# Padding the last tile of an MLP's inner layer to 128, first loads moved to ScalarE's ring, jumps moved to the ends of the queues

## Chip, cores and metric

The kernel runs on one core of a Trainium2 chip. The metric is the device time of one execution, in microseconds (us), as the median of several. Most executions of one kernel lie within a few tenths of a per cent of each other (the widest spread here is pad_jumps', 4.8 us of 1384, 0.34%).

## The reference

```python
mod = (silu(c) @ w_mod).reshape(1, 6, 1, 640)          # six modulation rows
sa, ca, ga, sb, cb, gb = ...
# attention: x is 2048 x 640, 32 heads of 128, K and V come from a cache of 2048 rows a head
#   q = h @ wq ; p = softmax(q k^T / sqrt(128)) ; o = p v ; out = o @ wo
# mixer MLP (on 640 columns):
#   x1 = x + shifted(gelu(layernorm(x) @ w1)) @ w2
#   out = x1 + gelu(layernorm(x1) @ w3) @ w4            # w3: 640 x 1728, w4: 1728 x 640
```

Two facts matter. The inner size of the MLP is 1728 = 13 x 128 + 64, so its last tile is half a tile. And before the first attention step can run, the modulation rows, the normalised and transposed first 512 rows of x (hT of chunk 0), wq of head 0, and K and V of head 0 must all be there.

## The kernel before

A planner written in Python puts every operation into the queue of one of five engines, in the order of keys given with each operation. A DMA is also an instruction in the queue of the engine that issues it: a load "on ScalarE" stands in ScalarE's queue between its ordinary work (in before two such issues took 0.39 and 0.54 us of it, see its timeline below). The functions the argument touches (cuts marked):

```python
# jumps: how many instructions each engine executes before its jump to the unrolled code
# (a negative number counts from the end of its queue)
FIRST = {"PE": 3, "ACT": 10000, "DVE": 0, "POOL": 7, "SP": -5}
HINT  = {"PE": 0, "ACT": -30, "DVE": 0, "POOL": 0, "SP": -12}
...
def load_v(h, prio, eng="SP", gate=(), need=()):        # 512 KB: 16 x 128 rows of 256 bytes
    dma(eng, lambda e: e.dma_start(V_ap[b][:, :, 0:128],
        A_v_cache[0, h].rearrange("(t p) d -> p t d", p=128)), 512, gate, (V[b],), prio, need)
...
dma("ACT", lambda e: e.dma_start(pre_ap, mod_src(2)), 800, (wm[1],), pre_t, -292)   # "pre": w_mod part 2
load_v(0, -290, "ACT", gate=(wm[1],))                                              # V of head 0
...                                                     # V of heads 1 to 3, wq, most of x, all K: on SyncE
def w3_part(ch, key):
    for f in range(NF):                                 # NF = 14; FS[13] = 64
        fs = FS[f]
        for kk in range(KT):                            # KT = 5
            PE: matmul(m[0:fs, :], w3_ap[:, kk, f*128 : f*128+fs], nT_ap[ch][:, kk, :])
        ACT: gT_ap[0:fs, f, :] = gelu(m[0:fs, :])
def w4_tile(t, key):
    for hf in range(2):
        for f in range(NF):
            PE: matmul(m[:, ...], gT_ap[0:fs, f, ...], w4_ap[f][0:fs, hf*HD:(hf+1)*HD])
```

## Time and profile before

| | before |
|---|---|
| median of the first three runs | 1391.6 us (1391.36 to 1391.62) |
| span of the profiled execution | 1391.3 us |
| TensorE busy | 1379.4 us, 99% |
| first S matmul, first P.V matmul | 18.11, 21.77 us |
| seventh query projection starts | 64.01 us |
| last output tile starts | 1384.17 us |

The page's first table and its chain of waits:

```profile
span 1391.3 us, 29861 instructions
...
PE 1379.4 (99%) x13128; PEld 941.2 (68%) x13128; DVE 539.6 (39%) x1401; ACT 1101.5 (79%) x1143; POOL 100.9 (7%) x88
...
PE 97%; DVE 1%; DMA 1%; SPq 0%; issue 0%; ACT 0%
```

TensorE is the limit nearly all the time. What can be won is where it stands, or is slow though busy. It stands only near the start. The timeline of TensorE there (start, duration, engine, line, operation, tiles, shapes, count, and in brackets the idle time before it with what ended it):

```profile
11.74 0.29 PE L448 MATMUL f_M<-f_s_bf,f_W 128*128 128x1 bf16 x6
13.38 0.25 PE L448 MATMUL f_M<-f_s_bf,f_W 128*128 128x1 bf16 x4 [1.34 <-issue]
...
14.85 2.34 PE L666 MATMUL f_M<-f_hT,f_wq 128*128 128x512 bf16 x5 [0.64 <-DVE f_hT L568]
...
18.11 0.59 PE L734 MATMUL f_S<-f_PQ,f_KV 128*128 128x512 bf16 x2
...
21.77 0.62 PE L753 MATMUL f_O<-f_KV,f_PQ 128*128 128x129 bf16 x8
...
49.17 0.61 PE L753 MATMUL f_O<-f_KV,f_PQ 128*128 128x129 bf16 x8 [1.94 <-DMA f_KV<-in_A_v_cache_dram]
55.84 1.24 PE L666 MATMUL f_M<-f_hT,f_wq 128*128 128x512 bf16 x5
64.01 1.24 PE L666 MATMUL f_M<-f_hT,f_wq 128*128 128x512 bf16 x5
```

Ten small matmuls are cut by 1.34 us in which TensorE waited for nothing that the profile shows ("issue"). Each step (one head, 512 rows of x) has one query projection (L666); two of them are 8.17 us apart when nothing is late (55.84 to 64.01, the sixth and the seventh). At 49.17 TensorE waited 1.94 us for a V. The chain of waits, in order of time, says whose and why (start, duration, what; SPq is SyncE's queue; L573 are transposes of hT):

```profile
38.59 0.99 SPq L573
...
43.04 1.26 SPq L583
44.35 4.69 DMA f_KV<-in_A_v_cache_dram
```

It is V of head 3, which was issued only when SyncE's transposes were through.

Near the end TensorE never idles, but the tiles with a 64-row matmul take longer. The timeline of the last output tiles, and TensorE's weight loads in the list of waits (total us, times, longest):

```profile
1379.95 4.29 PE L928 MATMUL f_M<-f_KV,f_OO 128*128 128x320 bf16 x28
1384.17 4.29 PE L928 MATMUL f_S<-f_KV,f_OO 128*128 128x320 bf16 x28
...
PEld f_M L928 <- issue: 7.0, 25, 0.4
PEld f_S L928 <- issue: 2.6, 10, 0.3
```

From tile to tile it is 4.22 us for 28 matmuls (1384.17 - 1379.95). The view merges them; two of each 28 have 64 rows.

### The profile page before, as it was taken

To read this page: it belongs to the slowest core of one execution; us is meant where nothing else is said; L and a number is where in the kernel's file an instruction comes from. 1 tells how busy PE (TensorE), PEld (TensorE's weight loads), DVE (VectorE), ACT (ScalarE), POOL (GpSimd) and SP (SyncE) were. 2 spreads that over 40 slices of the span, in tenths; PEclk is the share of its full clock that TensorE was granted. 3 is DMA by queue.
4 is the path that set the end of the run, shared out by engine and by line. 5 is a ranking of instruction groups with operands and counts; after the bars stand their busy time and mean duration, and the time that the engine had idled before them with its cause. 6 is when DMAs were issued, how large, how long until landed. Compare 5 with 4: busy or idle time off the path is not lost.

```text
span 1391.3 us, 29861 instructions
## 1 busy us (share of the span) xinstructions
PE 1379.4 (99%) x13128; PEld 941.2 (68%) x13128; DVE 539.6 (39%) x1401; ACT 1101.5 (79%) x1143; POOL 100.9 (7%) x88
## 2 busy tenths in 40 slices
PE   9999999999999999999999999999999999999999
PEld 6667767777777777777777776777776766645554
DVE  5453232333233322333233323332333245987553
ACT  5888888888888898888888888888888888732222
POOL 0000000000000000000000000000333248200000
PEclk9999999999999999999999999999999999999999
DMA  9651623161214221241205122612254102531210
GB/s 220 130 115 31 117 78 83 36 107 35 46 36 84 58 46 36 48 92 30 54 17 98 31 45 36 107 36 46 55 91 114 17 16 48 120 53 24 53 43 25
DMA packets 259179, 88.90 MB, mean 64 GB/s; under 512 B 236705, under 2 KB 257762, under 8 KB 259042
## 3 DMA queue, kind: packets, MB, share of 16 engines
q1 hardware_dynamic: 255762, 84.59, 30.7%
q10 hardware_dynamic: 3280, 2.33, 0.7%
q8 instruction: 105, 1.72, 0.5%
q14 instruction: 32, 0.26, 0.1%
HBM read 43.48 MB, written 2.62 MB: 33 GB/s over the span
## 4 chain that ended last, share of the span: by engine, by line
PE 97%; DVE 1%; DMA 1%; SPq 0%; issue 0%; ACT 0%
PE f_O L753 33%; PE f_S L734 31%; PE f_M L666 10%; PE f_M L691 10%; PE f_M L928 3%; PE f_S L914 2%; PE f_O L914 2%; PE f_S L928 2%; PE f_S L887 1%; PE f_S L864 1%; PE f_O L864 1%; PE f_M L887 1%; DMA f_W<-in_w_mod_dram 0%; DMA f_KV<-in_A_v_cache_dram 0%; SPq L573 0%; PE f_M L610 0%
## 5 line engine op out<-in xcount | busy, mean ns | idle before, releaser
L736 ACT ACTIVATE f_PQ<-f_S 128x1024 bf16<-128x1024 f32 x1024 | 1041.0, 1023 | 148.2 <-PE f_S L734 135.1
L753 PEld LDWEIGHTS f_O<-f_KV,f_PQ 128*128 128x128 bf16 x8192 | 589.4, 98 | 233.7 <-issue 2.4
L734 PE MATMUL f_S<-f_PQ,f_KV 128*128 128x512 bf16 x2048 | 726.9, 379 | 0.2 <-ACT f_PQ L736 0.2
L753 PE MATMUL f_O<-f_KV,f_PQ 128*128 128x129 bf16 x8192 | 713.0, 220 | 2.7 <-DMA f_KV<-in_A_v_cache_dram 1.9
L699 DVE TENSOR_TENSOR f_y<-f_M,f_y 128x320 f32<-128x320 f32 x192 | 94.3, 491 | 536.3 <-PE f_M L691 536.3
L691 PE MATMUL f_M<-f_wo,f_OO 128*128 128x320 bf16 x992 | 272.9, 299 | 0.0
L734 PEld LDWEIGHTS f_S<-f_PQ,f_KV 128*128 128x128 bf16 x2048 | 196.7, 97 | 30.5 <-ACT f_PQ L736 1.2
L666 PE MATMUL f_M<-f_hT,f_wq 128*128 128x512 bf16 x640 | 177.3, 381 | 1.1 <-DVE f_hT L568 0.6
L691 PEld LDWEIGHTS f_M<-f_wo,f_OO 128*128 128x128 bf16 x992 | 96.1, 98 | 28.5
L762 DVE TENSOR_TENSOR f_OO<-f_O,f_rl 128x256 bf16<-128x256 f32 x256 | 108.4, 423 | 8.1
L669 DVE CAST f_PQ<-f_M 128x512 bf16<-128x512 f32 x128 | 88.5, 691 | 56.9 <-PE f_M L666 56.8
L520 POOL TENSOR_TENSOR f_y<-f_y,f_mod 128x640 f32<-128x640 f32 x32 | 49.6, 1560 | 820.1 <-DVE f_y L699 819.9
L666 PEld LDWEIGHTS f_M<-f_hT,f_wq 128*128 128x128 bf16 x640 | 62.2, 98 | 65.9 <-DVE f_hT L575 1.5
L760 DVE RECIPROCAL f_rl<-f_O 128x2 f32<-128x2 f32 x256 | 43.4, 169 | 32.1 <-PE f_O L753 27.9
L928 PE MATMUL f_M<-f_KV,f_OO 128*128 128x320 bf16 (+1 forms) x308 | 47.1, 300 | 0.0
L917 ACT ACTIVATE f_OO<-f_O 128x512 bf16<-128x512 f32 (+1 forms) x28 | 16.6, 596 | 38.5 <-PE f_O L914 38.5
L526 ACT ACTIVATE f_xn<-f_y,f_small 128x640 bf16<-128x640 f32 x10 | 9.1, 915 | 41.6 <-DVE f_small L505 41.6
L928 PEld LDWEIGHTS f_M<-f_KV,f_OO 128*128 128x128 bf16 (+1 forms) x308 | 28.6, 97 | 18.7 <-issue 7.0
L697 DVE COPY f_y<-f_M 128x320 f32<-128x320 f32 x32 | 15.7, 490 | 63.5 <-PE f_M L691 63.5
L481 DVE BATCH_NORM_STATS2 f_small<-f_y 128x6 f32<-128x320 f32 x64 | 29.6, 480 | 2.0 <-POOL f_y L520 2.0
L917 ACT ACTIVATE f_OO<-f_S 128x512 bf16<-128x512 f32 (+1 forms) x28 | 16.7, 595 | 13.1 <-PE f_S L914 13.1
L942 DVE TENSOR_TENSOR f_y<-f_M,f_y 128x640 f32<-128x640 f32 x10 | 8.2, 825 | 43.2 <-PE f_M L928 43.2
(134 smaller groups left out, 513.9 us busy)
## 6 DMA issues: line engine op xcount, KB each, us to landing
f_KV<-in_A_v_cache_dram SPq DMA_DIRECT2D x31, 512.0 KB, 4.8
f_wo<-in_A_wo_dram SPq DMA_DIRECT2D x8, 640.0 KB, 4.4
f_xin<-in_A_x_dram SPq DMA_DIRECT2D x15, 320.0 KB, 4.6
f_wq<-in_A_wq_dram SPq DMA_DIRECT2D x7, 640.0 KB, 4.6
f_W<-in_w_mod_dram SPq DMA_DIRECT2D x3, 800.0 KB, 4.9
out_dram<-f_xin SPq DMA_DIRECT2D x15, 160.0 KB, 1.8
f_KV<-in_B_w_dram SPq DMA_DIRECT2D x5, 432.0 KB, 3.3
f_KV<-in_A_k_cache_dram SPq DMA_TRANSPOSE x128, 2.7
```

What stands on the lines that cost most here:

```text
L520: P.op(eng, lambda e: e.tensor_tensor(out=out, in0=a, in1=b, op=op), COST[eng][0], rd, wr, prio, lat=300 if eng == "POOL" else None)
L666: P.op("PE", lambda e, i=i, kk=kk: e.matmul(m.ap, wq_t[g % 2][:, kk, hh * 128:(hh + 1) * 128], hT_t[ch][:, kk, :], start=(i == 0), stop=(i ...
L669: P.op("DVE", lambda e: e.tensor_copy(q.ap, m.ap), 690, (m,), (q,), s * NP - 90)
L691: P.op("PE", lambda e, m=m, qt=qt, hf=hf, hh=hh: e.matmul(m[:, 0:HD], OT_ap[gs][:, qt, hh, :], wo_t[g % 2][:, hh, hf * HD:(hf + 1) * HD], ...
L699: P.op("DVE", lambda e, m=m, yt=yt: e.tensor_tensor(out=yt.ap, in0=m[:, 0:HD], in1=yt.ap, op=ALU.add), 490, (m, yt), (yt,), s * NP - 60)
L734: P.op("PE", lambda e, sp=sp, r=r, kt=kt: e.matmul(sp[:, r * QC:(r + 1) * QC], K_ap[b][:, kt * 128:(kt + 1) * 128], q.ap, start=True, stop ...
L736: x = P.op("ACT", lambda e, sp=sp, pt=pt: e.activation(pt.ap.rearrange("p k q -> p (k q)"), sp.ap, ACT.Exp, scale=SCALE), 1021, (sp,), (pt ...
L753: ins = e.matmul(o[bk][:, w * 129:w * 129 + 129], pt[:, r, qt * 128:(qt + 1) * 128], V_ap[b][:, u, 0:129], start=(u == 0 and w == 0), stop ...
L760: P.op("DVE", lambda e, ov=ov, i0=i0: e.reciprocal(rl_t[:, i0:i0 + 2].unsqueeze(2), ov[:, 0:258].rearrange("p (u d) -> p u d", u=2)[:, :, ...
L762: evac.append(P.op("DVE", lambda e, ov=ov, i0=i0, bk=bk: e.tensor_tensor(out=On_ap[gs][:, 2 * bk:2 * bk + 2, hh, :], in0=ov[:, 0:258].rear ...
L914: P.op("PE", lambda e, m=m, f=f, kk=kk, fs=fs: e.matmul(m[0:fs, :], w3_ap[:, kk, f * 128:f * 128 + fs], nT_ap[ch][:, kk, :], start=(kk == ...
L928: P.op("PE", lambda e, f=f, hf=hf, fs=fs: e.matmul(m[:, hf * 512:hf * 512 + HD], gT_ap[0:fs, f, i * 128:(i + 1) * 128], w4_ap[f][0:fs, hf ...
```

## The change

Its intent: (1) pad the inner layer to 14 x 128, so that no matmul has 64 rows; (2) get the first data in earlier by putting plain loads on ScalarE's ring and leaving SyncE the transposes; (3) move the engines' jumps so that the gap they are taken to cause doesn't fall into the start. The diff, cut to its core:

```diff
-    FIRST = {"PE": 3, "ACT": 10000, "DVE": 0, "POOL": 7, "SP": -5}
-    HINT = {"PE": 0, "ACT": -30, "DVE": 0, "POOL": 0, "SP": -12}
+    FIRST = {"PE": 100000, "ACT": 100000, "DVE": -6, "POOL": 100000, "SP": -5}
+    HINT = {"PE": -300, "ACT": -30, "DVE": -60, "POOL": -1, "SP": -12}
...  (the planner's DMA model and some costs: cut)
+        if ch == 1:                                  # x of chunk 1 in one load, on ScalarE
+            dma("ACT", lambda e: e.dma_start(y_t[:, 4:8, :]..., x2d[512:1024, :]...), 640, (), xs + held, -296.7, after=(wm_load[3], ln0[1]))
...
-    dma("ACT", lambda e: e.dma_start(pre_ap, mod_src(2)), 800, (wm[1],), pre_t, -292)
+    dma("ACT", lambda e: e.dma_start(pre_ap, mod_src(2)), 800, (wm[3],), pre_t, -297, after=(ln0[0],))
-         modulation(2, hf, ..., lambda k, hf=hf: (-262, 0.5)[hf] + 0.01 * k, -50)
+         modulation(2, hf, ..., lambda k, hf=hf: 0.5 + hf + 0.01 * k, -50)
-    load_v(0, -290, "ACT", gate=(wm[1],))
+    load_v(0, -296.5, "ACT", after=(ln0[1],))
+        if h in (1, 2, 3):
+            load_k(h, (-294, -291, -289)[h - 1], (wm[2],), () if h < 3 else from_slot(12))
+            load_v(h, (-293, -290, -289.5)[h - 1], "ACT" if h == 1 else "SP", ...)
-    load_wq(0, 1, HG, -295.985, gate=(wm[2],))
+    load_wq(0, 1, HG, -296.8, eng="ACT", after=(ln0[0],))
...
+    pad = T()
+    P.op("POOL", lambda e: e.memset(w3_ap[:, :, FF:FP], 0.0), 300, (), (pad,) + kv(2, 3, 4), E + 12)
+    P.op("DVE", lambda e: e.memset(w4_ap[NF - 1][FL:128, :], 0.0), 400, (), (pad,) + kv(4), E + 12, slack=500.0)
...
-            fs = FS[f]
-                ... e.matmul(m[0:fs, :], w3_ap[:, kk, f * 128:f * 128 + fs], nT_ap[ch][:, kk, :], ...
+                ... e.matmul(m.ap, w3_ap[:, kk, f * 128:(f + 1) * 128], nT_ap[ch][:, kk, :], ...
-                ... e.matmul(m[...], gT_ap[0:fs, f, ...], w4_ap[f][0:fs, ...], ...
+                ... e.matmul(m[...], gT_ap[:, f, ...], w4_ap[f][:, ...], ...
...  (order of the tail: three priorities and one list: cut)
```

"ScalarE's ring" stands here for the loads that ScalarE issues; their packets have one DMA queue to themselves in the trace (q10). It now carries, in this order: pre, wq of heads 1 to 3, x of chunk 1 (below: x1), V of head 0, V of head 1.

More of the change, by code (lines that the diff above doesn't have):

```diff
@@ L93, in schedule @@
         t_eng = {e: 0.0 for e in self.ENG}
-        dma_t = 0.0
+        dma_t = {e: 1600.0 for e in self.ENG}
         avail = {e: [] for e in self.ENG}
@@ L139, in schedule @@
             if o.dma:
-                dma_t = max(dma_t, s + o.dur) + o.kb * 1024 / 340.0
-                o.end = dma_t + 2000.0
+                t = max(dma_t[e], s + o.dur)
+                both = min(max(0.0, max(dma_t[x] for x in self.ENG if x != e) - t), o.kb * 1024 / 190.0)
+                dma_t[e] = t + both + (o.kb * 1024 - 190.0 * both) / 380.0
+                o.end = dma_t[e] + 2000.0
             else:
@@ L273, in fast_path @@
     FL = FF - (NF - 1) * 128
-    FS = [128] * (NF - 1) + [FL]
+    FP = NF * 128
     G4 = D // 4
@@ L365, in fast_path @@
     W3_OFF = 2 * KVW
-    w3_ap = KV_t[:, W3_OFF:W3_OFF + KT * FF].rearrange("p (k n) -> p k n", k=KT)
+    w3_ap = KV_t[:, W3_OFF:W3_OFF + KT * FP].rearrange("p (k n) -> p k n", k=KT)
     w3 = [T() for _ in range(KT)]
-    W4_HI = W3_OFF + KT * FF
+    W4_HI = W3_OFF + KT * FP
     NW4 = 12
@@ L415, in fast_path @@
     wm = [T() for _ in range(KT)]
+    wm_load = []
     for k in range(KT):
-        dma("ACT" if k % 2 else "SP", lambda e, k=k: e.dma_start(wm_ap[:, k, :], w_mod[k * 128:(k + 1) * 128, 0:2 * D]), 320, (), (wm[k],), -300 + 0.1 * k)
+        wm_load.append(dma("ACT" if k % 2 else "SP", lambda e, k=k: e.dma_start(wm_ap[:, k, :], w_mod[k * 128:(k + 1) * 128, 0:2 * D]), 320, (), (wm[k],), -300 + 0.1 * k))
     P.op("ACT", lambda e: e.preload_act_table_set(EXPSET), 1300, (), (), -295)
@@ L486, in rstd_act @@
         P.op("ACT", lambda e: e.activation(r, mv_ap[g][:, a:b, 1], ACT.Ln, bias=EPS), 220, tuple(mvs[g][a:b]), (rs[g],), prio, slack=slack)
-        P.op("ACT", lambda e: e.activation(r, r, ACT.Exp, scale=-0.5), 220, (rs[g],), (rs[g],), prio)
+        return P.op("ACT", lambda e: e.activation(r, r, ACT.Exp, scale=-0.5), 220, (rs[g],), (rs[g],), prio)
     def rstd_dve(g, a, b, prio):
@@ L514, in normed @@
                                               op0=ALU.subtract, op1=ALU.mult),
-             430 if fp else 240, (src_t, mvs[g][i], rs[g]), (dst_t,), prio)
-    COST = {"POOL": (1600, 950), "DVE": (825, 430)}
+             445, src_t + (mvs[g][i], rs[g]), (dst_t,), prio)
+    COST = {"POOL": (1600, 950), "DVE": (825, 590)}
     def tt(eng, out, a, b, op, rd, wr, prio):
@@ L532, in scaled @@
                  (src_t, rs[g], mvs[g][i]), (out_t,), prio)
-    XP, XS = (0, -294, -20, -20), (0, -1, 22, 44)
+    XP, XS = (0, -294.5, -20, -20), (0, -1, 22, 44)
+    ln0 = []
     def ln1(ch, prio):
         g = ln_slot()
-        xs = x0 if ch == 0 else load_x2(4 * ch, XP[ch], from_slot(XS[ch])) + load_x2(4 * ch + 2, XP[ch], from_slot(XS[ch]))
+        if ch == 1:
+            xs = tuple(T(y_t[:, t, :].bitcast(BF16)[:, 0:D]) for t in range(4, 8))
+            held = tuple(v for t in range(4, 8) for v in y[t])
+            dma("ACT", lambda e: e.dma_start(y_t[:, 4:8, :].bitcast(BF16)[:, :, 0:D], x2d[512:1024, :].rearrange("(t p) d -> p t d", p=128)),
+                640, (), xs + held, -296.7, after=(wm_load[3], ln0[1]))
+        else:
+            xs = x0 if ch == 0 else load_x2(4 * ch, XP[ch], from_slot(XS[ch])) + load_x2(4 * ch + 2, XP[ch], from_slot(XS[ch]))
+            held = ()
         for a, z in ((0, 2), (2, 4)) if ch < 2 else ((0, 4),):
             for i in range(a, z):
-                ln_stats(xs[i].ap, (xs[i],), g, i, prio, 0.0 if ch == 0 else 2000.0)
+                ln_stats(xs[i].ap, (xs[i],) + held, g, i, prio, 0.0 if ch == 0 else 2000.0)
             if ch == 0:
-                rstd_act(g, a, z, prio - 100)
+                ln0.append(rstd_act(g, a, z, prio - 100))
             else:
@@ L547, in ln1 @@
             for i in range(a, z):
-                normed(xn[i].ap, xn[i], xs[i].ap, xs[i], g, i, False, prio - 1)
+                normed(xn[i].ap, xn[i], xs[i].ap, (xs[i],) + held, g, i, False, prio - 1)
         raw = [T() for _ in range(4)]
@@ L576, in ln1 @@
                                                            scalar2=saT[:, k:k + 1], op0=ALU.mult, op1=ALU.add),
-                     210, tuple(raw) + (saT, caT), (hT[ch][k],), prio)
+                     400, tuple(raw) + (saT, caT), (hT[ch][k],), prio)
     def load_k(h, prio, gate=(), need=()):
@@ L583, in load_k, with load_v, load_wq @@
             dmaT(lambda e, i=i: e.dma_start_transpose(K_ap[b][:, i * 512:(i + 1) * 512].unsqueeze(1), A_k_cache[0, h, i * 512:(i + 1) * 512, :]),
-                 128, gate if i or h else (), (K[b][i],), prio + 0.01 * i, need)
-    def load_v(h, prio, eng="SP", gate=(), need=()):
+                 128, gate if i or h else (), (K[b][i],), prio + (1.6 if h == 0 and i else 0) + 0.01 * i, need)
+    def load_v(h, prio, eng="SP", gate=(), need=(), after=()):
         b = h % NKV
-        dma(eng, lambda e: e.dma_start(V_ap[b][:, :, 0:128], A_v_cache[0, h].rearrange("(t p) d -> p t d", p=128)), 512, gate, (V[b],), prio, need)
-    def load_wq(g, a, b, prio, need=(), gate=()):
-        dma("SP", lambda e: e.dma_start(wq_t[g % 2][:, :, a * 128:b * 128],
+        dma(eng, lambda e: e.dma_start(V_ap[b][:, :, 0:128], A_v_cache[0, h].rearrange("(t p) d -> p t d", p=128)), 512, gate, (V[b],), prio, need, after)
+    def load_wq(g, a, b, prio, need=(), eng="SP", after=()):
+        dma(eng, lambda e: e.dma_start(wq_t[g % 2][:, :, a * 128:b * 128],
                                         A_wq[:, (g * HG + a) * 128:(g * HG + b) * 128].rearrange("(k p) d -> p k d", p=128)),
-            160 * (b - a), gate, tuple(wq[g % 2][a:b]), prio, need)
+            160 * (b - a), (), tuple(wq[g % 2][a:b]), prio, need, after)
     def load_wo(g, prio, need=()):
@@ L600, in fast_path @@
     of_step = lambda s: (s // (NC * HG), s // HG % NC, s % HG)
-    load_wq(0, 0, 1, -297)
-    load_k(0, -296, gate=(wm[2],))
+    load_wq(0, 0, 1, -298)
+    load_k(0, -297.5, gate=(wm[2],))
     ln1(0, -280)
@@ L617, in fast_path @@
     pre_t = tuple(K[NKV - 1]) + (V[NKV - 1],)
-    dma("ACT", lambda e: e.dma_start(pre_ap, mod_src(2)), 800, (wm[1],), pre_t, -292)
+    dma("ACT", lambda e: e.dma_start(pre_ap, mod_src(2)), 800, (wm[3],), pre_t, -297, after=(ln0[0],))
     for hf in range(2):
-        modulation(2, hf, pre_ap, pre_t, "O%d" % hf, lambda k, hf=hf: (-262, 0.5)[hf] + 0.01 * k, -50)
+        modulation(2, hf, pre_ap, pre_t, "O%d" % hf, lambda k, hf=hf: 0.5 + hf + 0.01 * k, -50)
     v_ones(NKV - 1)
-    load_v(0, -290, "ACT", gate=(wm[1],))
+    load_v(0, -296.5, "ACT", after=(ln0[1],))
     def load_head(h):
@@ L627, in load_head @@
         n = first * NP - 14 if h < HG else (first - 12) * NP
-        load_k(h, pr, (wm[2],) if h == 1 else (), from_slot(n))
-        load_v(h, pr + 1, gate=(wm[2],) if h == 1 else (), need=from_slot(n + 1))
+        if h in (1, 2, 3):
+            load_k(h, (-294, -291, -289)[h - 1], (wm[2],), () if h < 3 else from_slot(12))
+            load_v(h, (-293, -290, -289.5)[h - 1], "ACT" if h == 1 else "SP", () if h == 1 else (wm[2],), after=(ln0[1],) if h == 1 else ())
+            return
+        load_k(h, pr, need=from_slot(n))
+        load_v(h, pr + 1, need=from_slot(n + 1))
     def load_group(g):
@@ L648, in fast_path @@
                        lambda k, i=2 * n + hf: NP * (MS + i) + 4.65 + k, NP * MS - 60)
-    TAIL = ("A0 B0 B1 A1 B2 B3 WO B4 B5 I3 A2 B6 C0 B7 D0 D1 D2 B8 D3 B9 C1 D4 A3 B10 B11 "
+    TAIL = ("A0 B0 B1 A1 B2 B3 WO B4 B5 I3 A2 B6 C0 B7 D0 D1 D2 B8 B9 D3 C1 A3 B10 B11 D4 "
             "B12 D5 B13 D6 B14 D7 B15 C2 D8 D9 D10 D11 C3 D12 D13 D14 D15").split()
@@ L653, in fast_path @@
     QUAD = (2, 3)
-    WOD, CH, I3D = -100, -1000, -200
+    WOD, CH, I3D = -200, -1000, 100
     evac, last_ot = [], []
@@ L838, in fast_path @@
     for k, old in ((0, kv(2)), (1, kv(2)), (2, kv(2, 3)), (3, kv(3)), (4, kv(3, 4))):
-        dma("SP", lambda e, k=k: e.dma_start(w3_ap[:, k, :], B_w3[k * 128:(k + 1) * 128, :]), 432, (), (w3[k],) + old, E + 5 + k)
+        dma("SP", lambda e, k=k: e.dma_start(w3_ap[:, k, 0:FF], B_w3[k * 128:(k + 1) * 128, :]), 432, (), (w3[k],) + old, E + 5 + k)
     for i, (f0, f1, old) in enumerate(((0, 6, kv(0)), (6, 12, kv(0, 1)))):
@@ L911, in w3_part @@
             m = Tile(pool="T")
-            fs = FS[f]
             for kk in range(KT):
-                P.op("PE", lambda e, m=m, f=f, kk=kk, fs=fs: e.matmul(m[0:fs, :], w3_ap[:, kk, f * 128:f * 128 + fs], nT_ap[ch][:, kk, :],
+                P.op("PE", lambda e, m=m, f=f, kk=kk: e.matmul(m.ap, w3_ap[:, kk, f * 128:(f + 1) * 128], nT_ap[ch][:, kk, :],
                                                                     start=(kk == 0), stop=(kk == KT - 1)),
-                     MM(QC), (w3[kk],) + tuple(nT[ch]), (m,), key + f + 0.1 * kk, accum=True)
-            P.op("ACT", lambda e, m=m, f=f, fs=fs: e.activation(gT_ap[0:fs, f, :], m[0:fs, :], GELU),
+                     MM(QC), (w3[kk], pad) + tuple(nT[ch]), (m,), key + f + 0.1 * kk, accum=True)
+            P.op("ACT", lambda e, m=m, f=f: e.activation(gT_ap[:, f, :], m.ap, GELU),
                  act(QC), (m,), (gT[f],) + (tuple(a for b in On + OT for a in b) if ch == 0 else ()), key + f)
@@ L926, in w4_tile @@
             for f in range(NF):
-                fs = FS[f]
-                P.op("PE", lambda e, f=f, hf=hf, fs=fs: e.matmul(m[:, hf * 512:hf * 512 + HD], gT_ap[0:fs, f, i * 128:(i + 1) * 128],
-                                                                 w4_ap[f][0:fs, hf * HD:(hf + 1) * HD], start=(f == 0), stop=(f == NF - 1)),
-                     MM(HD), (gT[f], w4_of(f), w4b), (m,), key + hf + 0.01 * f, accum=True)
+                P.op("PE", lambda e, f=f, hf=hf: e.matmul(m[:, hf * 512:hf * 512 + HD], gT_ap[:, f, i * 128:(i + 1) * 128],
+                                                                 w4_ap[f][:, hf * HD:(hf + 1) * HD], start=(f == 0), stop=(f == NF - 1)),
+                     MM(HD), (gT[f], w4_of(f), w4b, pad), (m,), key + hf + 0.01 * f, accum=True)
             if last:
```

## The prediction

> What bounds the kernel now. The first table has TensorE busy 1379.4 of 1391.3 us (99%); the chain of waits that ended last is 97% TensorE. ScalarE (79%), VectorE (39%) and DMA are not the limit on average. The change can only win (a) TensorE time that is slow though busy, (b) the few places where TensorE stands.
>
> (a) The MLP's inner size is 1728 = 13 x 128 + 64. In the groups by shape the 64-row matmuls take 307 ns against 300, but in the list of waits their weight loads have 9.6 us of idle put down to "issue" (35 times, about 0.26 us). The chain shows the price: an output tile's 28 matmuls of 320 columns take 4.22 us, while a w2 tile without partial tiles takes 1.36 us for 10, so 28 should take 3.82. That is four changes of row count, 0.10 us each; the inner layer's 64-column group loses as much at both ends (1.20 us against 1.08). In all 36 partial groups, two changes each: 7.3 us. [...] So padding should cost TensorE nothing. Expected -7.3 us, all critical: TensorE has no idle from 1242 us to its end.
>
> (b) Start. Steps take 8.17 us; from 36.78 to 56.00 two take 19.22: 2.9 us lost. The chain names transposes on SyncE's queue and, behind them, the V load of head 3, issued at 44.35. In the changed order that V goes out before these transposes, and the x rows come earlier on ScalarE's ring: -2.9 us.
> At 12.03 TensorE stands 1.34 us for "issue" amid ten matmuls. [...] With the jump at the queue's end it should go. But most is eaten: VectorE now copies the modulation before normalising rows 2 and 3, and modulation weights, wq, x, V of heads 0 and 1 queue in that order on ScalarE's ring. V of head 0 took 12.4 us to land; now it is issued near 11.5 us behind 1.9 MB, so the first P.V (21.8 us) may wait. Net -0.7 us, +-1.5.
>
> Added: two clears of padding (estimate 0.4 us each). VectorE's stands before an output release for which TensorE already waits 0.38 us (1201.99): +0.3. The stall at 1224 to 1234 us (about 3.9 us, VectorE's products and a lowered clock) keeps its order and stays. Later order changes meet no TensorE idle: 0. The end (2.8 us after the last matmul) stays.
>
> Sum: 1391.6 - 7.3 - 2.9 - 0.7 + 0.3 = 1381.0 us. Range 1378.5 to 1384. Faster by over 2%: 0.01; within 2%: 0.985; slower: 0.005.
>
> To check: output tiles 3.82 us in the chain, no "issue" idle before their weight loads; steps 3 and 4 at 8.2 us each, no wait for V of head 3; no 1.34 us gap near 12 us; when the first P.V starts.
>
> What would make it wrong: V of head 0 or wq late (start +1 to +3 us); a cost of late jumps at the end; a new wait on ScalarE or VectorE in the shortened MLP[...].

From 1391.6 us, -7.3 (padding), -2.9 (V of head 3), -0.7 (jumps, and the new order of loads) and +0.3 (VectorE's clear) come to 1381.0 us. The first term was worked out from the times of before (4.22 us measured for a tile's 28 matmuls against 3.82 scaled from 1.36 for 10). That padding adds no time of its own, and that the gap belongs to the early jump, were estimates.

## More of the kernel before

ScalarE's timeline shows two of its DMA issues (ACTq: pre, then V of head 0) and then the first eviction of hT (a copy of the transposed rows out of the matmul's output buffer):

```profile
7.18 0.39 ACTq L618 DMA_DIRECT2D f_KV<-in_w_mod_dram  x1
7.61 0.54 ACTq L588 DMA_DIRECT2D f_KV<-in_A_v_cache_dram  x1
...
14.25 0.78 ACT L564 ACTIVATE f_hT<-f_O,f_small 128x512 bf16<-128x512 bf16 x1 [3.02 <-PE f_M L559]
```

## The result

Ratios here and below are the mean time of one kernel's fast runs over that of the other's of the same rounds, so not quite the ratio of the medians.

| | before | after |
|---|---|---|
| median, us | 1391.48 (4 runs, 1389.35 to 1391.62) | 1390.32 (4 runs, 1389.25 to 1390.59) |
| ratio | | 0.9994, 95% interval 0.9976 to 1.0011 |
| profiled span, us | 1391.3 | 1389.2 |

The prediction was 1381.0 us with a range of 1378.5 to 1384: nine microseconds of gain did not come. The profile after, in the views of before. The page:

```profile
span 1389.2 us, 29853 instructions
...
PE 1372.7 (99%) x13128; PEld 945.8 (68%) x13128; DVE 540.6 (39%) x1402; ACT 1101.6 (79%) x1143; POOL 101.4 (7%) x89
```

TensorE's busy time fell by 6.7 us, and the span by only 2.1. TensorE's timeline at the start:

```profile
11.75 0.39 PE L451 MATMUL f_M<-f_s_bf,f_W 128*128 128x1 bf16 x10
...
14.28 0.84 PE L682 MATMUL f_M<-f_hT,f_wq 128*128 128x512 bf16 x2 [0.64 <-DVE f_hT L580]
21.23 1.46 PE L682 MATMUL f_M<-f_hT,f_wq 128*128 128x512 bf16 x3 [6.12 <-ACT f_hT L576]
23.48 1.03 PE L750 MATMUL f_S<-f_PQ,f_KV 128*128 128x512 bf16 x2 [0.79 <-DVE f_PQ L685]
...
29.06 0.62 PE L769 MATMUL f_O<-f_KV,f_PQ 128*128 128x129 bf16 x8
...
60.24 1.24 PE L682 MATMUL f_M<-f_hT,f_wq 128*128 128x512 bf16 x5
68.42 1.24 PE L682 MATMUL f_M<-f_hT,f_wq 128*128 128x512 bf16 x5
```

The ten small matmuls run without a gap, and from the first P.V to the seventh query projection it now takes 39.36 us against 42.24: the 2.9 us of V of head 3 are gone, as predicted. But TensorE stands 6.12 us for ScalarE's part of hT, and the first P.V comes 7.3 us later. When it went on, it was slower: the granted clock of TensorE was 0.50 from 20 to 26 us (in before it was 0.62 from 14 to 16 us, 0.53 from 16 to 18 and 1.00 after that), so a pair of S matmuls took 1.03 us in place of 0.59. The chain of waits says what held ScalarE:

```profile
10.42 0.21 ACTq L547
...
10.66 1.01 ACTq L600
...
11.71 8.64 ACTq L600
...
20.40 0.79 ACT f_hT L576
```

L547 is the load of x1, L600 twice the loads of V of heads 0 and 1. The mere issue of the second V held ScalarE for 8.64 us. The last transposing matmul, whose result it had to copy, had ended at 13.6 us.

The tail:

```profile
1378.18 3.97 PE L946 MATMUL f_M<-f_KV,f_OO 128*128 128x320 bf16 x28
1381.98 3.97 PE L946 MATMUL f_S<-f_KV,f_OO 128*128 128x320 bf16 x28
```

An output tile takes 3.80 us (predicted 3.82), and the "issue" waits of those weight loads are gone from the list. One more difference stands where attention ends. TensorE's timeline at the last P.V that waits for VectorE, before and then after:

```profile
1201.99 0.52 PE L753 MATMUL f_O<-f_KV,f_PQ 128*128 128x129 bf16 x6 [0.38 <-DVE f_OO L762]
```

```profile
1206.92 0.52 PE L769 MATMUL f_O<-f_KV,f_PQ 128*128 128x129 bf16 x6 [0.90 <-DVE f_OO L778]
```

Half a microsecond more: VectorE clears the padded rows of w4 just there (0.33 us at 1205.88).

Five marks cut both spans into stretches. Each mark is the start of a group of matmuls in TensorE's timeline; the "first w1 group after the stall" is the first of the mixer MLP's matmuls with w1 behind the two waits for VectorE at 1226 to 1236 us.

| stretch | before | after | difference |
|---|---|---|---|
| start to seventh query projection | 64.01 | 68.42 | +4.41 |
| to the last query projection | 1127.92 | 1127.92 | 0 |
| to the last P.V that waits for VectorE | 10.06 | 10.58 | +0.52 |
| to the first w1 group after the stall | 33.13 | 33.18 | +0.05 |
| to the last output tile | 149.05 | 141.88 | -7.17 |
| sum | | | -2.19 |

So the question is the start: why 4.4 us are lost where 3.6 were to be won.

### The profile page after: what moved, and what is told of

Read it like the earlier page. It is cut to its first block, busy times and chain, and to the rows that moved or that the text cites. A ratio compares the mean times of both kernels' runs of the same rounds, so it can differ in the third digit from the quotient of the medians.

```text
span 1389.2 us, 29853 instructions
## 1 busy us (share of the span) xinstructions
PE 1372.7 (99%) x13128; PEld 945.8 (68%) x13128; DVE 540.6 (39%) x1402; ACT 1101.6 (79%) x1143; POOL 101.4 (7%) x89
## 3 DMA queue, kind: packets, MB, share of 16 engines
q1 hardware_dynamic: 252498, 82.92, 29.9%
q10 hardware_dynamic: 6528, 4.00, 1.3%
## 4 chain that ended last, share of the span: by engine, by line
PE 97%; DVE 2%; ACTq 1%; ACT 0%; issue 0%; POOL 0%; POOLq 0%
PE f_O L769 33%; PE f_S L750 32%; PE f_M L682 10%; PE f_M L707 10%; PE f_M L946 3%; PE f_S L933 2%; PE f_O L933 2%; PE f_S L946 2%; PE f_S L907 1%; PE f_S L884 1%; PE f_O L884 1%; ACTq L600 1%; PE f_M L907 1%; DVE f_small L484 1%; PE f_M L622 0%; DVE f_y L805 0%
## 5 line engine op out<-in xcount | busy, mean ns | idle before, releaser
L936 ACT ACTIVATE f_OO<-f_O 128x512 bf16<-128x512 f32 x28 | 16.7, 596 | 48.1 <-PE f_O L933 48.1
L713 DVE COPY f_y<-f_M 128x320 f32<-128x320 f32 x32 | 15.7, 490 | 64.1 <-PE f_M L707 64.1
L946 PE MATMUL f_M<-f_KV,f_OO 128*128 128x320 bf16 x280 | 39.7, 299 | 0.0
L946 PEld LDWEIGHTS f_M<-f_KV,f_OO 128*128 128x128 bf16 x280 | 27.4, 98 | 11.0
L484 DVE BATCH_NORM_STATS2 f_small<-f_y 128x6 f32<-128x320 f32 (+1 forms) x72 | 32.9, 479 | 2.0 <-POOL f_y L523 2.0
L936 ACT ACTIVATE f_OO<-f_S 128x512 bf16<-128x512 f32 x28 | 16.6, 596 | 12.5 <-PE f_S L933 12.5
L946 PE MATMUL f_S<-f_KV,f_OO 128*128 128x320 bf16 x168 | 23.8, 299 | 0.0
```

The lines of the kernel that those rows point to most:

```text
L484: P.op("DVE", lambda e, hf=hf: e.bn_stats(s[:, hf * 6:hf * 6 + 6], src[:, hf * HD:(hf + 1) * HD]), 485, src_t, (s,), prio, slack=slack)
L946: P.op("PE", lambda e, f=f, hf=hf: e.matmul(m[:, hf * 512:hf * 512 + HD], gT_ap[:, f, i * 128:(i + 1) * 128], w4_ap[f][:, hf * HD:(hf + 1) ...
```

## The experiments

Theory A grew over the first runs into this, as an assumption to be tested: the issue of a load is held when too many pieces (contiguous rows) of earlier loads of the same engine are still outstanding. In after the issue of V of head 0 took 1.01 us, and that of V of head 1, behind the 2048 pieces of 256 bytes of V of head 0, 8.64 us. From the code, pre has 640 pieces, wq 640, x1 512: 1792 in front of V of head 0. The packets of ScalarE's queue (q10) in after's trace agree: 640 of 768 bytes (wq), 4096 of 256 bytes (two V), and 1408 of 1280 bytes (pre, x1 and 256 rows of x).

### v1_sync: V of head 1 from SyncE

```diff
-            load_v(h, (...)[h - 1], "ACT" if h == 1 else "SP", ...)
+            load_v(h, (...)[h - 1], "SP", (wm[2],))
```

> The changed kernel with the V load of head 1 issued from SyncE's queue (behind the K transposes of heads 0 and 1) instead of ScalarE's. Theory A (ScalarE stood 8.6 us in the issue of this load[...] and so wrote its two hT tiles at 20.4 us instead of about 13.7): ScalarE evicts hT at 13.7 to 14.3 us, the first P.V starts at 20 to 23 us instead of 29.1, and the time falls by 6 to 8 us to 1382 to 1384. Theory B (the start is limited by the bytes in flight, V of head 0 landing at about 24.6 us whatever ScalarE does): first P.V not before 24.5, time 1385.5 to 1387. Theory C (the late jumps or the order on VectorE cost the start): time stays at 1389 to 1391.

Measured: 1388.79 us (1387.15 to 1389.77), ratio 0.9982 (0.9969 to 0.9996). ScalarE's first hT eviction starts at 13.33 us in place of 20.40, the first S matmul at 16.22 in place of 23.48: the 8.64 us are indeed the issue of V of head 1. But TensorE's timeline has a new wait, for V of head 0, which landed 15.2 us after its issue behind the other loads:

```profile
26.05 1.03 PE L769 MATMUL f_O<-f_KV,f_PQ 128*128 128x129 bf16 x8 [5.49 <-DMA f_KV<-in_A_v_cache_dram]
```

So two walls stood one behind the other, and taking away the first wins only 3 us of the first P.V (29.06 to 26.05), and about 1.5 us of the median (medians of different rounds): after the 5.49 us the granted clock was low again (0.75 over 26 to 32 us, after 0.97 over 20 to 26), and the group above took 1.03 us in place of 0.62. The first P.V and the time that theory A expected were missed; on the first P.V, rival B was right.

### dummy_4kb and dummy_256b: another load in V of head 1's place

v1_sync with one load more at the old place of V of head 1: the same 512 KB, once in 128 pieces of 4 KB, once in 2048 pieces of 256 bytes, into a buffer not yet in use.

```diff
+    dma("ACT", lambda e: e.dma_start(<16 x 128 x 128 of a free buffer>, A_v_cache[0, 1].rearrange("(p t) d -> p t d", p=128)), 512, ...)   # 4 KB pieces
+    dma("ACT", lambda e: e.dma_start(<the same>,                         A_v_cache[0, 1].rearrange("(t p) d -> p t d", p=128)), 512, ...)   # 256 B pieces
```

> As v1_sync, and in the place where the changed kernel issued V of head 1 from ScalarE an extra load of the same 512 KB into memory nobody reads yet, in rows of 4 KB on both sides (128 pieces). Theory A in its form 'the ring holds a number of pieces[...]': the issue takes under 1 us, ScalarE evicts hT before 15 us, time within 1.5 us of v1_sync. Theory A in its form 'the ring holds a number of bytes or of transfers': the issue takes 7 to 9 us, hT at 20 us, time as the changed kernel, 1389 to 1391.

> The same extra 512 KB into the same place, but in rows of 256 bytes (2048 pieces), as V is loaded. Both forms of theory A: the issue takes 7 to 9 us and the time is 1389 to 1391. If it is under 2 us here too, the length of the issue belonged to V of head 1 itself (its wait or its place) and not to the ring.

Measured: the extra load's issue was held 8.49 us in the first and 8.43 us in the second; hT evictions at 20.13 and 19.74 us; times 1389.36 (ratio 0.9987) and 1390.36 us (0.9995). The pieces of the load that is held make no difference. That form of the theory fell. What was left is that the load in front, V of head 0, makes it wait.

### dummy4kb_first and dummy256_first: the same load in front of V of head 0

The same two loads, now between x1 and V of head 0. One execution each.

> Kernel after with V1 loaded by SyncE and an extra load of 512 KB in 4 KB rows (128 pieces) put on ScalarE's ring between x1 and V0. Theory A[...]: pre 640 + wq 640 + x1 512 + 128 = 1920 pieces still fit, V0's issue is short as in v1_sync (under 1.5 us), nothing is issued behind it, and ScalarE's first hT eviction starts at 13 to 14 us. Rival B (the bytes that stand in the ring decide): 512 KB more in the ring ahead of V0 holds V0's issue for about 8 us and the hT evictions move to about 20 us. In either case V0 itself lands later than in v1_sync (25.9 us), and the time is worse than v1_sync's by 1 to 4 us.

> The same extra 512 KB, in 256 B rows (2048 pieces) between x1 and V0. Theory A: the extra load takes V0's place[...], so V0's issue is the one that is held for about 8 us or more, and ScalarE's first hT eviction starts at about 20 us. Rival B (bytes): the same as in the run with 4 KB rows. The two runs differ only in the number of pieces, so if one is held and the other is not, pieces decide; if both are held, bytes or the mere count of transfers decide.

ScalarE's timeline with the 4 KB pieces (L634 is the extra load, L600 V of head 0):

```profile
10.69 0.80 ACTq L634 DMA_DIRECT2D f_y<-in_A_v_cache_dram  x1
11.53 0.70 ACTq L600 DMA_DIRECT2D f_KV<-in_A_v_cache_dram  x1
13.04 0.78 ACT L576 ACTIVATE f_hT<-f_O,f_small 128x512 bf16<-128x512 bf16 x1 [2.63 <-PE f_M L571]
```

and with the 256-byte pieces:

```profile
10.63 0.54 ACTq L634 DMA_DIRECT2D f_y<-in_A_v_cache_dram  x1
11.21 8.90 ACTq L600 DMA_DIRECT2D f_KV<-in_A_v_cache_dram  x1
20.16 0.78 ACT L576 ACTIVATE f_hT<-f_O,f_small 128x512 bf16<-128x512 bf16 x1 [9.74 <-issue]
```

The same bytes, the same place, the same issue behind them. Behind a load of 128 pieces it takes 0.70 us, behind one of 2048 pieces 8.90. In this pair the number of pieces ahead decides (1920 in all against 3840, by the code), not their bytes. Rival B fell. Nor did the hold stop SyncE's queue: in after SyncE issued four more transposes during ScalarE's 8.64 us. The first kernel lost its time elsewhere, as expected: TensorE waited 4.5 us for V of head 0 there.

### x1_sync: x1 from SyncE, both V stay on ScalarE

```diff
-            dma("ACT", lambda e: e.dma_start(y_t[:, 4:8, :]...
+            dma("SP", lambda e: e.dma_start(y_t[:, 4:8, :]...
```

> Kernel after with x of chunk 1 loaded by SyncE in place of ScalarE; V0 and V1 stay on ScalarE's ring. Theory A: the 512 pieces of x1 are gone from in front of V0, so[...] V1's issue holds ScalarE only until about 16 to 17.5 us, not 20.4; hT evictions start at 16 to 18 us; time about 1387 to 1389 us. Rival C (V1's issue waits for something else that comes at 20 us whatever lies ahead of V0): hT evictions at 20 us again and the time as after, 1390.

```profile
10.21 6.86 ACTq L600 DMA_DIRECT2D f_KV<-in_A_v_cache_dram  x2
17.12 0.78 ACT L576 ACTIVATE f_hT<-f_O,f_small 128x512 bf16<-128x512 bf16 x1 [6.71 <-issue]
```

Measured: 1387.41 us (1386.99 to 1387.81), ratio 0.9973 (0.9956 to 0.9990). ScalarE is free at 17.1 us, as theory A expected. Here wq is the last load ahead of V of head 0; it was issued at 8.33 and took 8.9 us to land, so it landed at 17.2. In after that last load is x1: issued at 10.22, 10.3 us to landing, so 20.5, and ScalarE was free at 20.35. In both kernels ScalarE comes free when what stands in front of V of head 0 has landed. The packet records of all seven kept traces with a held issue say it more sharply: the hold ended 0.34 to 0.38 us after the last packet of the loads in front of the first 256-byte load had ended, at 16.69 us (x1_sync) to 22.82 us (loads_only), while only 420 to 673 of that load's own 2048 packets had. Rival C fell.

By the number of pieces in front (from the code) the issues of V and of the extra loads read: 640 pieces 0.54 us (before), 1920 pieces 0.70 us (dummy4kb_first), 3328 pieces 6.44 us (x1_sync), 3840 pieces 8.64 us (after), 8.90 (dummy256_first) and 8.49 and 8.43 (dummy_4kb and dummy_256b). Where between 1920 and 3328 pieces the hold begins was not measured, and why there is one was not shown. It is no small part of a load's time: in after 8.64 us, against 13.9 and 15.7 us from issue to landing of the two V loads.

### loads_only: the loads and the order without padding and late jumps

The padding and the jump constants undone in after; nothing else.

> Kernel after without the padding and without the late jumps: the loads and the order alone. If the parts add up, this is slower than before by what the padding gained and after lost: after stands at 0.9994, the padding alone gives 0.9949, so about 1396 to 1398 us (ratio 1.004 to 1.006), with the first S matmul at about 23 to 25 us and the step marks about 4 to 6 us later than before's. Rival: the loss comes from padding and loads together (the extra memsets, other order), then it is below 1394.

Measured: 1398.48 us (1395.32 to 1398.75), ratio 1.0044 (1.0027 to 1.0061). hT evictions at 23.22 us after two V issues of together 12.38 us, first S at 26.31. The loads alone cost 6 us and more; the stretch at the end of attention is 10.06 us as in before, so the new order of the tail costs nothing there. The rival (below 1394) fell; first S and step marks (the seventh projection at 71.76 us) came still later than expected.

### pad_only: the padding alone

The padding put into before; nothing else.

> The kernel before with the padding and its two clears alone: order of loads, jumps and priorities as before. Theory (padding is worth 7.3 us, and the changed kernel lost it again at the start): output tiles 3.80 us, time lower by 6.5 to 7.5 us, 1384 to 1385. Rival (the gain in the tail needs the new tail order, or is given back to a wait on VectorE or ScalarE): 1387 to 1391.

Measured: 1383.89 us (1383.13 to 1384.78), ratio 0.9949 (0.9936 to 0.9963). The last stretch is 141.88 us as in after. Padding alone is better than the whole change by 6.4 us. Its profile also shows two things that matter below. The "issue" gap at 12 us was 2.92 us long here, not 1.34, and with a start so delayed TensorE no longer waited for V of head 3. And the stretch with the stall was 1.6 us shorter than in before (31.50 against 33.13): the clock stayed up. The stretches' table of before and then of pad_only at the stall (window, then busy times, then the granted clock as a share of full speed, DMA share, GB/s):

```profile
1230.00:1232.00 2.00, 2.00 (x9) 1.13 (x8) 1.95 (x8) 0.00 (x0) 0.00 (x0) 0.50 0.78 153
```

```profile
1230.00:1232.00 2.00, 2.00 (x17) 1.43 (x16) 1.62 (x7) 0.00 (x0) 0.00 (x0) 1.00 0.56 111
```

Of the 16 kernels' profiles, only those of before, after and best2 had the low clock at that place (0.50 in the lowest 2 us of each). It comes and goes with the same waits in front of it; what decides was not shown. It is a term of 1.6 us that sits in some runs and not in others.

### no_dve_clear: after without VectorE's clear

```diff
-    P.op("DVE", lambda e: e.memset(w4_ap[NF - 1][FL:128, :], 0.0), 400, (), (pad,) + kv(4), E + 12, slack=500.0)
```

> Kernel after without VectorE's clear of the padded rows of w4 (what stands there is old finite K and V data, and it is multiplied by the exact zeros of the padded inner columns, so the result stays correct). Theory: the clear stood in front of an output release that TensorE waits for, and cost 0.5 us: the stretch from the last query projection of the attention to the first matmul of the modulation in the tail, 10.42 us in after and 9.90 in before, is 9.9 to 10.0 again; time -0.5 us, 1389.8 +- 0.5. Rival: the stretch is longer because of the other order of the tail, and stays at 10.4.

```profile
1207.53 0.52 PE L769 MATMUL f_O<-f_KV,f_PQ 128*128 128x129 bf16 x6 [0.38 <-DVE f_OO L778]
```

The wait is 0.38 us again. Counted from the start of the group, as in the table above, the stretch is 10.07 us against 10.58 (the expectation counted from 0.16 us later in both). The clear costs 0.5 us, as in pad_only, which has the 0.90 us wait too. In the time it did not show: 1390.51 us (ratio 0.9994); the profiled execution reached the seventh query projection 1.1 us later than after's. Half a microsecond is below what such medians tell; the trace tells it.

### jumps_only: the late jumps alone

```diff
-    FIRST = {"PE": 3, "ACT": 10000, "DVE": 0, "POOL": 7, "SP": -5}      (and HINT)
+    FIRST = {"PE": 100000, "ACT": 100000, "DVE": -6, "POOL": 100000, "SP": -5}
```

> Kernel before with only the later jumps (the constants of the change for where each engine's jump and its hint stand). Theory: the 1.34 us in which TensorE stood for 'issue' amid ten matmuls at 12 us [...] disappears, and since the matmuls behind it wait for VectorE's copies anyway only a part of it reaches the first S matmul: 0 to -1.3 us, time 1389.6 to 1391. Rival: the gap has another cause and stays, or turns up at another place of the start; time as before within 0.3 us. No cost at the queues' ends: the last VectorE instruction ends the span as before.

Measured: 1392.63 us (1391.35 to 1395.39), ratio 1.0006 (0.9992 to 1.0020): nothing won, and slower than expected. The gap did disappear, so it goes with the early jumps: it was 1.34 us in before, 0.80 in loads_only and 2.92 in pad_only, which have them, and is gone with the late ones. What it consists of was not shown, and of which engine's jump it comes was not tested apart. In the profiled execution, the slowest of the five, TensorE waited 3.2 us for the modulation weights instead (they landed 12.4 us after issue, against 8.2 in before), and 2.1 us for V of head 3.

### best2, pad_jumps and best3: where is V of head 3's 2.9 us?

All three are before with padding (POOL's clear alone) and late jumps. pad_jumps is only that. In best2 and best3 V of head 3 is issued earlier:

```diff
+        if h == 3:
+            load_v(h, -289.5, gate=(wm[2],))                                  # best2: ahead of V of head 1
+            load_v(h, -268, gate=(wm[2],), need=from_slot(n - NP + 1))        # best3: right behind V of head 2
```

> Built on before: its own loads, with only V of head 3 issued ahead of the transposes of hT of chunk 1; padding with the POOL clear alone; late jumps. The parts should add up: padding -7.1 us (run pad_only), no VectorE clear about -0.5, V of head 3 in time -2 to -2.9, jumps 0 to -1.3: 1379 to 1381.5 us, ratio 0.9915 to 0.993. Rival: V of head 3 early only moves the wait to hT of chunk 1 (0.26 us there before, at most 0.6 more): then 1381.5 to 1383.

> Kernel before with the padding (POOL's clear alone) and the later jumps, its own loads: run best2 without the V of head 3. Theory D (an absolute wall): V of head 3 is issued only when SyncE's transposes are through, at 44 to 46 us whatever TensorE does before, so the microsecond that the late jumps win near 12 us is waited away there or earlier for a load: the time is that of padding alone less the 0.5 us of VectorE's clear, 1383 to 1384.5 us, ratio 0.9945 to 0.9955, and the list of waits shows V of head 3 (about 1.5 to 3 us). Rival: the jumps are worth their 1.3 us: 1381.5 to 1382.8, ratio below 0.994. Also to be seen: whether TensorE again waits about 3 us for the modulation weights at the start, as in run jumps_only (then that is the rule and not an accident of one execution).

> The same with V of head 3 issued right behind V of head 2 (in best2 it went in front of V of head 1 and its second neighbour was issued behind it, and TensorE then waited 2.35 us at head 1). Theory D: the 2.35 us go, the wall of V of head 3 is away, and the next wall is hT of chunk 1 (VectorE's copies at 45.5 us in best2), so not all of it is won: 1381.5 to 1383 us, ratio 0.993 to 0.994, about 1 to 2 us better than pad_jumps. Rival: nothing is won against pad_jumps (within 0.4 us) because another load of SyncE's queue comes late in its place.

Measured: best2 1383.76 us (1382.23 to 1384.76), ratio 0.9943; pad_jumps 1383.87 (1381.87 to 1386.63), ratio 0.9956 (0.9943 to 0.9970); best3 1385.92 (1383.99 to 1386.75), ratio 0.9959. None is told apart from padding alone (0.9949), and my expectations for best2 and best3 were misses. In pad_jumps TensorE waits 2.1 us for V of head 3, in best2 2.35 us, by my reading for V of head 1 (it landed at 30.6 us, just before the matmul at 30.78; the profile names a VectorE instruction that ended then and whose result that matmul doesn't read), in best3 3.75 us for hT of chunk 1. SyncE's timeline says why. First pad_jumps, then best3 (L588 are V loads, L583 and L573 transposes of K and hT):

```profile
29.44 0.59 SPq L588 DMA_DIRECT2D f_KV<-in_A_v_cache_dram  x1
...
35.46 5.24 SPq L573 DMA_TRANSPOSE f_hT<-f_xn  x4
```

```profile
29.75 2.71 SPq L588 DMA_DIRECT2D f_KV<-in_A_v_cache_dram  x2
...
38.11 6.49 SPq L573 DMA_TRANSPOSE f_hT<-f_xn  x4
```

And TensorE in best3:

```profile
46.50 2.53 PE L669 MATMUL f_M<-f_hT,f_wq 128*128 128x512 bf16 x5 [3.75 <-DVE f_hT L575]
```

One V takes 0.59 us of SyncE's queue; two in a row take 2.71, so the second cost 2.1. It looks like the same effect as on ScalarE, smaller (not tested apart), and everything behind it on the queue, here the hT transposes, is late by as much and more. SyncE's queue is full from 4 to 46 us, and whichever of V and hT goes later is waited for. So the 2.9 us are no reserve of V of head 3 alone. That after wins them in its trace because its start is so late that SyncE has caught up, and because V of head 1 is off SyncE, is how I read it; pad_only, which starts late and has no such wait with before's order, speaks for it, but I did not test it alone.

What stays open: with before's loads the late jumps make the times spread more (pad_jumps over 4.8 us, jumps_only over 4.0, against 1.7 for pad_only). The landing of the modulation weights differs between the profiles (12.4 us in jumps_only, 6.9 in pad_jumps, in its fastest execution), which may be the reason; I did not isolate it.

### best1: little on ScalarE's ring

after with ScalarE's ring left to wq and V of head 0, V last; x1, pre and V of head 1 on SyncE behind the first transposes; the matmuls of pre spread over the first steps; no VectorE clear.

```diff
-            dma("ACT", ...x1..., -296.7, after=(wm_load[3], ln0[1]))
+            dma("SP",  ...x1..., -295.2, after=(wm_load[3], ln0[1], kops[0, 3]))
-    dma("ACT", lambda e: e.dma_start(pre_ap, mod_src(2)), 800, (wm[3],), pre_t, -297, after=(ln0[0],))
+    dma("SP",  lambda e: e.dma_start(pre_ap, mod_src(2)), 800, (wm[3],), pre_t, -294.5, after=(ln0[0], kops[0, 3]))
-         modulation(2, hf, pre_ap, pre_t, "O%d" % hf, lambda k, hf=hf: 0.5 + hf + 0.01 * k, -50)
+         modulation(2, hf, pre_ap, pre_t, "M", lambda k, hf=hf: NP * (1 + hf) + 4.65 + 0.7 * k, -50)
-    load_v(0, -296.5, "ACT", after=(ln0[1],))
+    load_v(0, -296.5, "ACT", after=(ln0[0],))
-            load_v(h, (...)[h - 1], "ACT" if h == 1 else "SP", ...)
+            load_v(h, (...)[h - 1], "SP", (wm[2],))
-    P.op("DVE", lambda e: e.memset(w4_ap[NF - 1][FL:128, :], 0.0), ...)
```

> Built on after to leave ScalarE's ring room: only wq and V0 go there (V0 last, so nothing is issued behind it), V1, x of chunk 1 and the modulation weights go to SyncE's behind the first transposes; padding, late jumps kept; no VectorE clear. Theory A: ScalarE's hT evictions start at 13 to 14 us, V0 is issued with 640 pieces ahead and lands by about 20 us, so the first P.V starts at 20 to 22 us and the step marks stand 0 to 2 us before those of the kernel before less its 2.9 us: time 1379.5 to 1382 us, ratio 0.991 to 0.9935. Rival: with more on SyncE's ring the K transposes of the first heads come late and TensorE waits for K in steps 0 to 2: 1383 or more.

```profile
7.88 0.54 ACTq L602 DMA_DIRECT2D f_KV<-in_A_v_cache_dram  x1
...
12.77 0.78 ACT L576 ACTIVATE f_hT<-f_O,f_small 128x512 bf16<-128x512 bf16 x1 [2.63 <-PE f_M L571]
```

Measured: 1382.12 us (1381.73 to 1382.33), ratio 0.9933 (0.9919 to 0.9946). The median is 0.1 us above the range that theory A expected, the ratio is within it, and the rival (1383 or more) fell. It beats before by 9.2 us (medians of the same rounds) and after by 8.2 (medians of different rounds), has the lowest median of all and the narrowest spread of the kernels with at least five runs. V of head 0 lands 8.0 us after its issue, the first P.V is at 21.59 us, and the seventh query projection at 62.31 against 64.01 in before. Its first S came 1.7 us earlier than before's, its first three steps take 8.85 us each because of the spread modulation, so there is still something to be had. Against pad_only the gain is not large: 1.8 us by the medians. The nearest kernel is pad_jumps (also late jumps, no VectorE clear, but before's loads): 1.75 us by the medians, of different rounds, and the intervals of the ratios touch (0.9919 to 0.9946 against 0.9943 to 0.9970). So what the new loads and tail are worth beyond padding is small and not firmly measured.

## Why the prediction was wrong

Point by point:

- "Expected -7.3 us, all critical." Right: 149.05 to 141.88 us, -7.17, the same in pad_only; without partial tiles the weight loads no longer wait for "issue", and an output tile takes 3.80 us. The waiting was not a matter of longer loads: in before one took 93 ns with 64 rows and 98 with 128. The waits of those loads came to 9.6 us in before and are not in after's list, where all loads use all 128 rows. Why a change of the row count makes a load wait was not shown.
- "VectorE's stands before an output release [...]: +0.3." Right in place; the size was 0.5 us (10.06 to 10.58). The 0.4 us it estimated is the cost that the code gives the planner; the clear itself took 0.33 us.
- "In the changed order that V goes out before these transposes [...]: -2.9 us." In the trace right (-2.88 us from the first P.V to the seventh query projection), as an item that adds to others wrong: best2 and best3 show that an earlier V of head 3 with before's loads only moves the wait.
- "With the jump at the queue's end it should go. But most is eaten." Right: the gap is gone, the first query projection of after starts only 0.57 us earlier (14.28 against 14.85) behind a new wait of 0.68 us for VectorE's normalising, and jumps_only wins nothing (1.0006).
- **The step that failed: "V of head 0 took 12.4 us to land; now it is issued near 11.5 us behind 1.9 MB, so the first P.V (21.8 us) may wait. Net -0.7 us, +-1.5."** I saw the queue of loads as a matter of landing times, and put 1.5 us on it. In its place the runs showed two walls. First, V of head 1's issue held ScalarE itself for 8.64 us, and with it the evictions of hT that TensorE needed (v1_sync, x1_sync, dummy256_first). Second, behind that, V of head 0 landed so late (24.6 us in after, 25.9 in v1_sync) that the first P.V had to be some 3 to 4 us late anyway. The first P.V came 7.3 us later, at 29.06 us, which is 8.0 us from the -0.7 predicted. The text even named the order of the five loads; what was missing was that an issue is an instruction in the queue of an engine with other work.
- "later order changes meet no TensorE idle: 0": right, 1127.92 us in both.
- The cut risk, another clock near 1230 us (+-1.5 us): exists, 1.6 us (0.50 in before against 1.00 in pad_only), but struck the profiles of both before and after (0.50 in each) and explains no difference between them.

The sum with measured terms: -7.2 + 0.5 - 2.9 + 7.3 = -2.3 us, the trace's -2.19 with the 0.05 of the stall. Had only the start been as predicted, this sum would give 1381 to 1382 us, within the range; but that counts the -2.9 us in full, which best2 and best3 put in doubt for an early start. best1, which mends the start, measured 1382.12.

## What to carry to other kernels

Issuing a load on a compute engine is not free of risk: here one issue held ScalarE for 8.64 us. Put only loads there that don't hold it (here up to 1920 pieces in front held nothing, and 3328 or more did), the one with very many short rows last, and nothing behind it that another load or urgent work of that engine would wait for. When you cost a new order of loads, write down for each issue what that engine does next, not only when the data lands. And measure the parts of a mixed change apart: here the padding alone was 6.4 us better than the whole.
